# The local mask copied on another engine, and a new order for the first 400 steps

## The chip, the cores and the metric

The kernel runs on one core of one Trainium2 chip. The metric is the device time of one execution in microseconds (us), the median of several runs. The core has five engines that each work through their own queue in order: TensorE (PE, matrix products and transposes into PSUM; its weight loads are shown apart as PEld), VectorE (DVE), ScalarE (ACT), GpSimd (POOL, which reads and writes SBUF only) and SyncE (SP, which here issues nearly all DMA transfers). They wait for each other through semaphores.

## The reference

Two layers. The first is attention over 8 batches, 8 heads, 576 tokens, head size 64: heads 0 to 3 see the last 32 tokens (`mask_local`), heads 4 to 7 every 32nd token before them (`mask_strided`). The second is a mixture of four causal attention experts over the result `x` (512 wide); each token uses its best two.

```python
scores = scale * np.matmul(q, k.transpose(0, 1, 3, 2))
mask_local = (rel >= 0) & (rel < stride)
mask_strided = (rel >= 0) & (pos[None, :] % stride == pos[:, None] % stride)
attn = softmax(np.where(mask, scores, -1e9)); x = attn @ v
logits = x @ w_gate; topk = the best 2 of 4 experts; w = softmax of those two
for e in range(E):
    q, k, v = x @ wq[e], x @ wk[e], x @ wv[e]
    a = softmax(causal(scale * q @ k.T)); ye = a @ v @ wo[e]
    out += w(e) * ye
```

## The kernel before, in words

The program is a list of 2579 steps (`op(...)`, each with a kind, the engines that may do it, what it reads and writes, and a function that issues its instructions). `schedule()` issues them in the order that the list `ORDER` gives; a step that two engines can do goes to the second of them if its number is in `SECOND`. Since every engine works in order, `ORDER` sets the queue of each engine, SP's too. `FILL` gives some step numbers a count of filler matmuls (L305, 512 columns into a free PSUM bank, nobody reads them), issued on PE just ahead of that step. What stands ahead of `schedule()` (masks, zeroing, L355 to L400) is placed into the queues by the program's own scheduler, between the steps.

The first layer works on pairs of heads (`stage1(b, hp)`): pairs 0 and 1 are local, 2 and 3 strided. Batch 0 starts cold. For one local pair of batch 0 the steps are: load q and k (SP, L537, 288 KB each); transposes on PE into a bank (`tp`: four for q, four for k at L611, two for the last block of both at L624); ten copies of these banks into `qkt` (`tp_out`, L345, ACT or DVE); 72 score matmuls (`sl`, L673), which need all ten copies; then for each head mask (DVE L703, adds `m_loc`), maximum (DVE L714), subtract (POOL L716), exp (ACT L718), sum (DVE L720); reciprocal (DVE L723, L725); scale (POOL L727); a transposition on DVE (`ptl`, L743); the value products (`xal`, PE L783, needs v, loaded by L589); and a split into a rounded part and a rest (`xh` ACT L765, `xl` DVE L767). A strided pair is alike, with `tp` at L640, scores `s` at L689, `pt` on PE at L753 and value products `xa` at L802. The copies of one head and one operand write interleaved columns of `qkt`, so a later one waits for an earlier one even on another engine.

The second layer multiplies `x` with the weights: `pj` (L977 in batch 0 for the first two experts, in parts of three matmuls, each part for one pair; L966 otherwise), `vp` (L895); the weights are loaded, rounded (`hi_w`, ACT L455) and the rest taken (`lo_w`, POOL or DVE, L457).

Step numbers: 0 to 4 are GpSimd's fills (causal mask, swapped mask, last rows, two lists of zero pads). Pair 0 of batch 0: 5, 6 load q and k; 7 `tp` of q with copies 8 to 11; 12 `tp` of k with copies 13 to 16; 17 the last block with copies 18, 19; 20, 21 load v; 22 `sl`; 23, 24 mask; 25, 26 maximum; 27, 28 subtract; 29, 30 exp; 31, 32 sum; 33 reciprocal; 34, 35 scale; 36 `ptl`; 37 `xal`; 38 to 45 the split; 46, 47 small copies (`xf`). Pair 1 is the same from 48 on (48, 49 loads; 50, 55, 60 `tp`; 51 to 54, 56 to 59, 61, 62 copies; 63, 64 v; 65 `sl`; 66, 67 mask; 70, 71 subtract; 72, 73 exp; 77, 78 scale; 79 `ptl`; 80 `xal`). Pair 2 is 91 to 127 (102 `s`, 119 `xa`), pair 3 128 to 164 (134, 136, 130, 132 `tp`; 139 `s`; 153 `pt`; 156 `xa`). 165 to 203 are the weights (185 the gate's), 204 on is batch 1 (pair 0 from 204 with `tp` 206, 211, 216 and `sl` 221; pair 1 from 242 with `tp` 244, 249, 254 and `sl` 259). 1136 to 1139 and 1143 to 1146 are the eight parts of the first key projection.

The mask itself, before:

```python
for i in (0, 2, 3, 4):
    nc.vector.tensor_copy(m_loc[:, i], m_loc[:, 1])
nc.vector.memset(m_loc[0:32, 0], 0.0)
keep(m_loc[0:32, 0], [[-1, 64]], 0, 1)
```

Of the kernel before, what the change touches and what calls it, by code (L numbers as in the profile page):

```python
# [22 lines left out]
def attention_moe_kernel(  # L23
# [20 lines left out]
    nc = tc.nc  # L44
# [39 lines left out]
    class Ring:  # L84
# [36 lines left out]
    }  # L121
    ORDER = [
# [136 lines left out]
    ]  # L259
    FILL = {  # L260
        7: 1, 17: 7, 80: 4, 132: 3, 134: 3, 139: 1, 216: 2,
    }

    def op(kind, eng, key, fn, r=(), w=(), mode=None, dmas=(), after=()):
# [100 lines left out]
    m_loc = const.tile([128, 5, 64], F32, name="m_loc")  # L365
# [11 lines left out]
    for i in (0, 2, 3, 4):  # L377
        nc.vector.tensor_copy(m_loc[:, i], m_loc[:, 1])
# [916 lines left out]
```

## Time and profile before

| | |
|---|---|
| median of 3 runs | 423.1 us (422.42 to 423.28) |
| the profiled execution | 422.69 us, of which the span from first to last instruction is 421.0 us |
| mean granted TensorE clock | 0.999 |
| busy, share of the span | PE 98%, PEld 85%, DVE 81%, ACT 66%, POOL 55% |

The profiled execution's own time is 1.7 us longer than its span; that remainder lies around the program and isn't touched here. "Busy" of PE counts a matmul until its modelled end, some 0.15 us after the next may start.

### The profile page before, as it was taken

The numbers are of one execution on the slowest core, as the hardware profiler recorded it, in microseconds if no ns is written. First come the engines' busy times: TensorE is split into PE (matmuls) and PEld (weight loads), VectorE is DVE, ScalarE is ACT, GpSimd is POOL, SyncE is SP. The second block draws the span as 40 slices with busy tenths as digits, with TensorE's granted clock in tenths as the row PEclk, the third lists the DMA queues.
The fourth block names the chain that finished last, engine by engine and source line by source line (L and its number), as shares of the span: only waits on it lengthen the run. The fifth ranks groups of instructions, "written<-read, shape, count | busy, mean of one in ns | idle before, by whom it ended". The sixth has DMA issues, their size and how long they took to land.

```text
span 421.0 us, 18647 instructions
## 1 busy us (share of the span) xinstructions
PE 411.0 (98%) x7523; PEld 358.8 (85%) x7523; DVE 339.8 (81%) x1073; ACT 277.5 (66%) x877; POOL 230.3 (55%) x398
## 2 busy tenths in 40 slices
PE   8889999999999999999999999999999999999996
PEld 5668988987898879998899888998899888997775
DVE  4897898999998899978976699898988896339840
ACT  5677378668776457877767465765666469657862
POOL 5674673776536750699229630589216671185540
PEclk9999999999999999999999999999999999999999
DMA  6667637554656655464356524750443040001033
GB/s 178 194 192 181 121 91 136 100 89 96 112 102 109 146 126 87 94 129 103 72 90 133 134 46 114 129 107 11 114 102 97 20 116 22 2 26 27 27 101 100
DMA packets 156502, 41.86 MB, mean 99 GB/s; under 512 B 146080, under 2 KB 149792, under 8 KB 156416
## 3 DMA queue, kind: packets, MB, share of 16 engines
q1 hardware_dynamic: 156272, 40.54, 43.9%
q8 instruction: 59, 0.97, 1.0%
q14 instruction: 27, 0.22, 0.2%
q10 hardware_dynamic: 144, 0.13, 0.1%
HBM read 31.20 MB, written 9.44 MB: 97 GB/s over the span
## 4 chain that ended last, share of the span: by engine, by line
PE 86%; DVE 5%; ACT 3%; DMA 2%; issue 1%; POOL 1%; SPq 0%; ACTq 0%; POOLq 0%
PE bank L966 22%; PE bank L1217 12%; PE bank L1183 10%; PE bank L895 10%; PE bank L1144 6%; PE bank L1059 5%; PE bank L783 3%; PE bank L802 3%; PE bank L1047 2%; PE bank L689 2%; PE bank L673 2%; PE bank L1081 2%; PE bank L753 2%; PE bank L977 1%; DMA p<-in_q_dram 1%
## 5 line engine op out<-in xcount | busy, mean ns | idle before, releaser
L1021 ACT ACTIVATE p<-p,st 128x384 f32<-128x384 f32 (+3 forms) x128 | 71.5, 561 | 10.8 <-DVE st L1016 10.7
L1117 POOL TENSOR_SCALAR p<-p,st,wt 128x256 f32<-128x256 f32 (+2 forms) x96 | 63.9, 672 | 15.1 <-DVE st L1108 7.4
L1016 DVE CUSTOM_DVE_ANT_0 p<-bank,m_cau 128x384 f32<-128x384 f32 (+2 forms) x96 | 50.0, 548 | 1.2 <-PE bank L1059 0.6
L1183 PE MATMUL bank<-th,vs 128*64 128x192 f32 (+4 forms) x512 | 48.0, 337 | 0.0
L563 DVE STREAM_TRANSPOSE qkt<-nat 128x576 f32<-128x576 f32 x48 | 47.5, 1002 | 0.1
L1183 PEld LDWEIGHTS bank<-th,vs 128*64 128x64 f32 x512 | 33.8, 137 | 13.8 <-issue 7.1
L345 ACT COPY th<-bank 128x256 f32<-128x256 f32 (+2 forms) x108 | 40.4, 434 | 7.6 <-PE bank L1144 7.2
L765 ACT CAST xh<-bank 128x128 fp32r<-128x128 f32 (+4 forms) x112 | 29.4, 320 | 22.3 <-PE bank L783 12.8
L966 PE MATMUL bank<-xh,wh_k 128*128 128x256 f32 (+1 forms) x120 | 36.3, 303 | 0.0
L895 PE MATMUL bank<-wh_v,xh 128*128 128x260 f32 x128 | 36.2, 283 | 0.0
L895 PE MATMUL bank<-wl_v,xh 128*128 128x260 f32 x128 | 36.2, 283 | 0.0
L966 PE MATMUL bank<-xh,wh_q 128*128 128x256 f32 (+1 forms) x120 | 36.1, 301 | 0.1
L767 DVE TENSOR_TENSOR xl<-bank,xh 128x128 fp32r<-128x128 f32 (+4 forms) x112 | 31.8, 322 | 5.3 <-ACT xh L765 5.0
L895 PE MATMUL bank<-wh_v,xl 128*128 128x260 f32 x128 | 35.9, 281 | 0.0
L966 PE MATMUL bank<-xl,wh_k 128*128 128x256 f32 (+1 forms) x120 | 35.5, 296 | 0.0
L966 PE MATMUL bank<-xh,wl_k 128*128 128x256 f32 (+1 forms) x120 | 35.5, 296 | 0.0
L966 PE MATMUL bank<-xl,wh_q 128*128 128x256 f32 (+1 forms) x120 | 35.5, 296 | 0.0
L966 PE MATMUL bank<-xh,wl_q 128*128 128x256 f32 (+1 forms) x120 | 35.5, 296 | 0.0
L1144 PEld LDWEIGHTS bank<-ident,p 64*128 64x128 f32 x800 | 30.2, 139 | 5.7 <-issue 1.3
L716 POOL TENSOR_TENSOR p1l<-p1l,st 128x640 f32<-128x640 f32 (+1 forms) x18 | 20.7, 1151 | 25.7 <-DVE st L714 25.5
L1144 PE MATMUL bank<-ident,p 64*128 64x64 f32 x800 | 33.7, 226 | 0.5 <-DVE p1l L703 0.3
L727 POOL TENSOR_TENSOR p1l<-p1l,st 128x640 f32<-128x640 f32 (+1 forms) x18 | 20.5, 1141 | 18.6 <-DVE st L725 15.2
(190 smaller groups left out, 1220.1 us busy)
## 6 DMA issues: line engine op xcount, KB each, us to landing
nat<-in_q_dram SPq DMA_DIRECT2D x96, 72.0 KB
nat<-in_k_dram SPq DMA_DIRECT2D x96, 72.0 KB
out_dram<-ys SPq DMA_DIRECT2D x23, 256.0 KB
v<-in_v_dram SPq DMA_DIRECT2D x96, 40.0 KB
out_dram<-ys SPq DMA_DIRECT2D x25, 128.0 KB
v<-in_v_dram SPq DMA_DIRECT2D x48, 54.0 KB
v<-in_v_dram SPq DMA_DIRECT2D x32, 48.0 KB
v<-in_v_dram SPq DMA_DIRECT2D x32, 45.0 KB
```

Source lines behind the costliest of these rows:

```text
L345: (nc.scalar.copy if e == "ACT" else nc.vector.tensor_copy)(dst, src)
L563: op("tq", {"DVE": 0.66 if local else 1.11}, k0 - 13, lambda e, x=x: nc.vector.transpose(turned(qkt.t, x), raw(x) if local else raw(x).rea ...
L765: op("xh", {"ACT": act(n_) + 0.04 * (not local)}, key, lambda e, s_=s_, x_=x_: nc.scalar.copy(x_(xh.t), s_(xa.t)), r=[xa], w=[xh[u]])
L767: op("xl", {"DVE": dve(n_)}, key + 0.5, lambda e, s_=s_, x_=x_: nc.vector.tensor_sub(x_(xl.t), s_(xa.t), x_(f(xh.t))), r=[xa, xh[u]], w=[x ...
L895: nc.tensor.matmul(vp.t[:, :NV], xx.t[:, t0:t0 + 128], ww.t[:, kt, :], start=i == 0, stop=i == 11)
L966: nc.tensor.matmul(pj.t[:, :n_], ww.t[:, kt, ep * 128:(ep + 1) * 128], xx.t[:, c], start=i == 0, stop=i == 11)
L1016: op("max2", {"DVE": 0.08 + 0.00104 * nk}, k_ + 0.5, lambda e, a=a: nc.vector.tensor_tensor_reduce(out=p.t[:, a, :nk], in0=sp[a].t[:, so:s ...
L1021: op("exp2", {"ACT": 0.285 + 0.00084 * nk}, k_ + 1, lambda e, a=a: nc.scalar.activation(p.t[:, a, :nk], p.t[:, a, :nk], AF.Exp, bias=st.t[ ...
L1117: lambda e, p=p, a=a, ci=ci, t=t, nk=nk, s_=s_, ep=ep: nc.gpsimd.tensor_scalar(p.t[:, a, :nk], p.t[:, a, :nk], s_.t[:, 20 + ci + a:21 + ci ...
L1144: nc.tensor.transpose(tp[hf].t[:, 64 * c:64 * c + 64], src, ident[r, r])
L1183: nc.tensor.matmul(acc.t[o, c0:c0 + cn], vw, th[ep, a].t[:, s0:s0 + cn], start=j == 0, stop=j == nj - 1, skip_group_check=True)
L1217: nc.tensor.matmul(yp.t[:, :n_], xx.t[:, c0:c0 + 128], ww.t[:, ep, c], start=i == 0, stop=i == 5)
```

## The change

Three things. GpSimd, not VectorE, makes the copies of the local mask: one copy of 64 columns, one of 192 columns (three blocks at once), and the memset. The order is another one up to about position 400 of the list (after that the two lists differ only in neighbours that swap places, up to position 980), with other engines for some steps in that stretch. The 21 fillers stand ahead of other steps.

```diff
     ORDER = [
-        3, 48, 49, 50, 55, 57, 59, 60, 56, 62, 58, 52, 54, 185, 5, 7, 61, 53, 9, 51, 8, 64, 6, 17, 19, 63, 12, 13,
-        16, 0, 11, 65, 66, 68, 70, 18, 67, 15, 129, 134, 10, 14, 69, 135, 72, 22, 136, 71, 73, 137, 128, 132, 133,
-        74, 92, 91, 130, 131, 1, 139, 24, 23, 26, 28, 97, 98, 95, 99, 25, 27, 29, 75, 76, 205, 93, 211, 215, 30,
-        96, 140, 141, 143, 20, 77, 78, 79, 145, 142, 31, 144, 32, 33, 35, 34, 147, 100, 149, 146, 148, 94, 80, 87,
-        150, 151, 81, 83, 84, 82, 212, 165, 168, 213, 214, 36, 204, 216, 217, 102, 166, 104, 106, 103, 88, 152,
-        153, 167, 154, 206, 208, 155, 210, 85, 86, 105, 218, 21, 37, 42, 43, 38, 44, 243, 249, 169, 1144, 40, 41,
-        45, 108, 107, 138, 156, 242, 209, 39, 110, 112, 253, 109, 111, 161, 1136, 1137, 251, 250, 113, 157, 158,
+        3, 2, 49, 55, 58, 56, 48, 50, 53, 59, 54, 51, 60, 62, 61, 6, 12, 13, 52, 57, 65, 67, 63, 66, 68, 0, 4, 70,
+        15, 69, 5, 7, 8, 11, 9, 17, 18, 10, 19, 72, 74, 64, 16, 129, 134, 135, 92, 71, 73, 75, 76, 77, 78, 136,
+        137, 14, 22, 23, 24, 25, 27, 79, 128, 130, 131, 205, 132, 133, 139, 211, 212, 97, 26, 99, 141, 143, 28, 98,
+        145, 140, 142, 144, 1, 30, 32, 80, 87, 29, 31, 33, 146, 148, 215, 21, 91, 93, 95, 147, 149, 100, 150, 185,
+        94, 96, 213, 83, 35, 34, 36, 102, 104, 88, 84, 152, 204, 103, 105, 214, 85, 165, 168, 151, 153, 81, 82,
+        166, 167, 155, 20, 37, 106, 206, 216, 169, 40, 41, 243, 249, 38, 39, 86, 1137, 44, 42, 154, 45, 209, 107,
+        109, 138, 156, 1144, 43, 111, 1136, 1143, 108, 110, 112, 253, 113, 115, 210, 217, 250, 218, 159, 160, 208,
...
     FILL = {
-        7: 1, 17: 7, 80: 4, 132: 3, 134: 3, 139: 1, 216: 2,
+        65: 4, 93: 2, 102: 4, 130: 1, 134: 6, 139: 1, 153: 3,
     }
...
-    for i in (0, 2, 3, 4):
-        nc.vector.tensor_copy(m_loc[:, i], m_loc[:, 1])
-    nc.vector.memset(m_loc[0:32, 0], 0.0)
+    nc.gpsimd.tensor_copy(m_loc[:, 0], m_loc[:, 1])
+    nc.gpsimd.memset(m_loc[0:32, 0], 0.0)
+    nc.gpsimd.tensor_copy(m_loc[:, 2:], m_loc[:, 1:2].to_broadcast([128, 3, 64]))
     keep(m_loc[0:32, 0], [[-1, 64]], 0, 1)
```

The changes of `SECOND` give these steps another engine. Copies of transposed banks go from ACT to DVE: 10, 18, 51, 56, 58, 61, 100, 135, 137, 251, 252, 253 and four later ones; from DVE to ACT: 8, 13, 16, 53, 118, 208, 210, 245, 248 and three later ones. `lo_w` of 172, 174, 190 and 197 goes from POOL to DVE. The key's rounded copies (`k_h`) 1141, 1148, 1180 and 1184 go from ACT to POOL, `k_l` 1142 from DVE to POOL. Five small copies out of PSUM go from DVE to ACT.

## Rows read from the trace of the kernel before

**Rows 1.** Busy time per stretch: engines in order, granted clock, DMA share, GB/s.
```profile
5.00:30.00 25.00, 22.08 (x571) 15.86 (x573) 20.53 (x59) 18.78 (x54) 14.87 (x34) 1.00 0.67 188
10.00:30.00 20.00, 17.23 (x547) 12.73 (x534) 18.43 (x51) 14.89 (x45) 13.16 (x26) 1.00 0.66 188
30.00:60.00 30.00, 29.76 (x628) 27.73 (x607) 25.71 (x72) 16.74 (x50) 17.94 (x31) 1.00 0.63 142
60.00:350.00 290.00, 288.66 (x5578) 256.39 (x5565) 255.44 (x779) 195.55 (x629) 164.23 (x254) 1.00 0.49 100
```

**Rows 2.** Timeline of the first 13 us: start, length, engine, line, [idle before, releaser].
```profile
1.71 0.43 SPq L469 DMA_DIRECT2D w_gate<-in_moe_w_gate_dram  x1
...
2.18 0.51 SPq L537 DMA_DIRECT2D p<-in_q_dram  x1
2.73 1.87 SPq L589 DMA_DIRECT2D v<-in_v_dram  x4
...
3.91 1.94 PE L611 MATMUL bank<-ident,p 128*128 128x128 f32 x8
...
6.01 0.54 DVE L378 COPY m_loc<-m_loc 128x64 f32<-128x64 f32 x4 [3.24 <-POOL m_loc L362]
...
6.79 0.78 PE L611 MATMUL bank<-ident,p 128*128 128x128 f32 x4
6.92 0.23 POOL L362 TENSOR_SCALAR_AFFINE_SELECT m_loc<-m_loc 32x64 f32<-32x64 f32 x1
...
7.41 1.67 PE L305 MATMUL bank<-ident 128*128 128x512 bf16 x7
...
8.42 2.68 DVE L345 COPY qkt<-bank 64x256 f32<-64x256 f32 x6 [1.81 <-ACT qkt L345]
...
9.80 0.97 PE L673 MATMUL bank<-qkt 64*32 64x64 f32 x72
...
12.32 1.54 POOL L716 TENSOR_TENSOR p1l<-p1l,st 128x320 f32<-128x320 f32 x2 [5.18 <-DVE st L714]
```

**Rows 3.** Timeline, PE and DVE: where the later steps of the start begin.
```profile
11.96 1.39 PE L673 MATMUL bank<-qkt 64*32 64x64 f32 x72 [0.15 <-ACT qkt L345]
...
16.36 1.33 PE L640 MATMUL bank<-ident,nat 108*128 108x108 f32 x12
...
18.21 0.85 DVE L743 STREAM_TRANSPOSE pt<-p1l 128x640 f32<-128x640 f32 x1 [0.32 <-POOL p1l L727]
...
19.74 1.11 PE L783 MATMUL bank<-pt,v 32*64 32x32 f32 x84 [0.64 <-ACT qkt L345]
...
21.63 0.81 PE L689 MATMUL bank<-qkt 64*54 64x54 f32 x44
...
26.56 0.42 PE L977 MATMUL bank<-xh,wh_k 128*128 128x320 f32 x1
...
29.70 0.97 PE L673 MATMUL bank<-qkt 64*32 64x64 f32 x72 [0.46 <-ACT qkt L345]
...
34.56 0.97 PE L673 MATMUL bank<-qkt 64*32 64x64 f32 x72 [0.18 <-DVE qkt L345]
```

**Rows 4.** Groups by line and shape, DVE, ACT and POOL, 0 to 30 us.
```profile
L345 DVE COPY qkt<-bank 64x256 f32<-64x256 f32 x9 | 3.8, 426 | 2.1 <-ACT qkt L345 1.8
L703 DVE TENSOR_TENSOR p1l<-bank,m_loc 128x320 f32<-128x320 f32 x4 | 1.8, 482 | 0.0
L345 ACT COPY qkt<-bank 64x256 f32<-64x256 f32 x19 | 7.8, 417 | 5.3 <-PE bank L611 4.4 <-DVE qkt L345 0.6
L716 POOL TENSOR_TENSOR p1l<-p1l,st 128x320 f32<-128x320 f32 x4 | 2.8, 722 | 5.9 <-DVE st L714 5.8
```

**Rows 5.** Groups by line and shape, POOL, the whole span: the nearest row to the mask's copies.
```profile
L821 POOL CAST xfh<-xh 128x64 fp32r<-128x64 f32 x18 | 4.1, 235 | 10.9 <-ACT xh L765 10.9
```

**Rows 6.** Timeline around the one `lo_w` that DVE does before 60 us.
```profile
35.89 0.74 POOL L457 TENSOR_TENSOR wl_q<-th,wh_q 128x256 fp32r<-128x256 f32 x1 [3.96 <-ACT wh_q L455]
...
36.09 0.82 DVE L457 TENSOR_TENSOR wl_q<-th,wh_q 128x256 fp32r<-128x256 f32 x1
```

174 rows, old and new, of tables (ORDER, SECOND) are left out of this document.

## The prediction

> **What bounds the kernel now.** I read the busy time per stretch first [rows 1]. From 60 to 350 us PE is idle 1.34 us of 290, from 30 to 60 us 0.24 of 30: there PE sets the time, and as the change leaves its products alone, nothing can be won in that part. The cold start is different: from 5 to 30 us PE is idle 25.00 − 22.08 = 2.92 us, and in the same stretch stand the 21 fillers. So the question is only how much useful PE work each version has done when PE becomes saturated near 30 us; a lead or a lag at that point is handed down to the end. The ceiling of a gain is those 2.92 us.
>
> In the start DVE is the engine behind PE's waits: 18.43 of 20 us busy between 10 and 30 us [rows 1], the rest being hardly more than the hops between 51 groups. ACT and POOL have slack. The timeline of the first microseconds [rows 2] shows why DVE comes late: it stands for 3.24 us, until 6.01, at the mask's copies, which wait for POOL's selects, and then at its first copy out of PSUM, which waits 1.81 us for an ACT copy of the same head. The first scores run at 9.80 us, the first subtract at 12.32.
>
> **The change, part by part.** I follow the new queues step by step with these durations [rows 4]: copy 0.43 on DVE, 0.42 on ACT; mask, maximum and sum 0.48 (0.42 to the next DVE start, as they overlap), subtract and scale 0.72, a hop to another engine 0.05. A filler takes 0.215 to the next start (7 in 1.67 with the last one's tail [rows 2]), a strided `tp` 0.33 (four in 1.33 [rows 3]), a local one 0.47 when the start is over.
>
> *The mask.* VectorE loses 0.54 us of copies and a memset of 0.11 [rows 2]. In the order of before this would give nothing: DVE would only stand longer at the copy that starts at 8.42. In the new order DVE is wanted from 4.95 us, when k of pair 1 (now loaded and transposed first) is through its four transposes (half of the 1.94 us from 3.91 [rows 2]). With the mask still on DVE its copies would begin at 6.01 + 0.54 + 0.11 = 6.66, 1.7 us later; so here the edit is a condition for the new order. On POOL the copies aren't in the trace. From below: 0.235 each, the POOL row for 64 columns [rows 5]; from above the 0.72 of a two-input operation of 320 columns [rows 4]. I take 0.24 and, for three times the columns, 0.45, with 0.11 for the memset as on DVE. POOL ended the mask at 7.15 [rows 2]; the five fills of step 2, at 0.235 each 1.2 us, may now stand ahead of it, so it ends at 7.15 + 0.8 + 1.2 = 9.15, or 9.9 with the upper price for both copies. It is wanted at 9.46 (below). Value taken: nothing, being nearest to the 64-column row.
>
> *The head.* PE has both operands of pair 1 through at 5.85 [rows 2]. DVE copies 58 and 56 at 4.95 and 5.38; ACT 53 and 59 from 5.89 to 6.73; DVE 54 and 51 to 6.80; ACT 62 to 7.08; DVE 61 to 7.15. Then ACT comes to 13, which needs k of pair 0. This load is third on SP now, in the place at 1.71 of the gate's weights, 0.47 us earlier than the load at 2.18 that PE waited for until 6.79 [rows 2]; like that one it has a v load right behind it: 6.3 us. Its `tp` ends about 7.1, ACT does 13, 52, 57 until 8.39, and the scores of pair 1 start at 8.44: 1.36 us earlier than 9.80. Mask, mask, maximum on DVE from 9.46, subtract on POOL at 10.95 instead of 12.32. The head wins 1.4 us, and pair 1's chain wins more: exp at 11.7, its scale ends 15.6, the transposition on DVE starts 15.9 instead of 18.21, the value products 18.1 instead of 19.74 [rows 3].
>
> *What pays for it.* Pair 0 waits. Its q is loaded behind a v load, its `tp` runs after the first scores (9.4 to 10.05), and the last two copies stand on ACT behind pair 1's two exps: its scores start at 13.6 instead of 11.96 [rows 3], and six fillers and two `tp` cannot fill PE to there (1.1 us idle). The strided pair 3 follows at 16.15, before 15.61. Pair 2's scores need copies that stand on ACT behind pair 1's `xh` and two exps and on DVE behind sums: 22.25 instead of 21.63 [rows 3], 1.0 us idle. After that pt of pair 3 at 24.1, `xal` of pair 0 at 24.5 (0.2 earlier than before), and the first `pj` at 27.15, behind an `xl` that DVE reaches last, instead of 26.56 [rows 3].
>
> *The balance.* At the scores of batch 1's pair 0 I get 30.15 against 29.70 [rows 3], but with one `pj` part and one `tp` more done ahead of them (0.50 + 0.24 us): a lead of 0.29. At the scores of pair 1 35.45 against 34.56, with one `pj` part (0.50) more done: a lag of 0.39, since ACT does two `xh` ahead of the copy that they need. Until the last parts of the key's projection 0.12 of it comes back (a `tp` of 0.33 is done by then, where before it follows): **a lag of 0.27 us**, say 0.3. The fillers are 21 in both, so they cancel as far as PE has no other work; the loads up to there are the same number.
>
> *After 37 us.* The work on POOL's `k_h` and on ACT isn't on PE's path as long as 30 to 60 us has 4.3 us of DVE, 13.3 of ACT and 12.1 of POOL idle [rows 1]. Four more `lo_w` go to DVE. The only one that it did before took 0.82 us, beside a POOL operation that began 0.20 us earlier and ended 0.54 us after it started [rows 6]; DVE's other time for 256 columns is 0.43. So they add 1.7 to 3.3 us to DVE, and I take the cover of 4.3 us as enough: nothing. The Trainium skill, "SBUF — State Buffer", section "SBUF: two separate sides", says that VectorE and GpSimd share one pair of SBUF ports as an exclusive lock, and that a VectorE instruction with two SBUF inputs blocks while a GpSimd instruction that reads SBUF holds it. The trace agrees: 0.82 less the 0.54 leaves 0.28 of work. By that rule the four would cost DVE the upper price whenever POOL is busy; without it the lower.
>
> The sum, against the profiled execution: 422.69 + 0.3 = 423.0 us. That execution lies 0.41 below the median of 423.1, so for a median I say 423.4.
>
> **The rivals.** What a measurement of this kernel can tell from no change is about 0.2%, 0.85 us.
>
> *The head's gain lasts (faster).* If pair 0's scores and pair 2's don't leave PE empty, because their loads and copies come a little earlier than I walk them, the two idle stretches of 1.1 and 1.0 us shrink. For it: DVE starts 3.5 us earlier, and the ceiling of 2.92 us leaves room. Against: the ACT queue, where 14 stands behind both exps whatever DVE does. With 1.4 us kept less the 0.27 of the walk's end and some fillers left without a free bank: 423.1 − 1.4 = 421.7; both stretches gone, 421.3. It decides if pair 2's scores start before 21.2 us.
>
> *DVE runs out of cover (slower).* By the shared SBUF access of [rows 6] the four `lo_w` take 0.82 each, 3.3 us, in the stretch from 36 to 50 us, where the value weights must be ready before the `vp` products. DVE has 14% idle between 30 and 60 us [rows 1], 2.0 us in 14. The excess of 1.3 us and the 0.3 of the sum stand in PE's way: 423.1 + 1.6 = 424.7. It decides if PE waits over 0.5 us for `lo_w` between 36 and 50 us.
>
> *The mask comes late (slower).* If POOL takes 0.72 for each of the five fills and both copies, the mask is ready at 7.15 + 3.6 + 1.55 = 12.3 instead of 9.46, and pair 1's chain slides by 2.8 us; half of that is hidden, since pair 0's scores wait for other copies: 423.4 + 1.4 = 424.8. It decides from 10.3 us on, and is seen as DVE idle at L703 with POOL as releaser. The Trainium skill, "GPSIMD Engine Reference", section 4.1, calls GpSimd roughly line-rate on one input and about twice as slow on two. No more than that is needed to make the 0.72 too high for copies; but the row of 0.235 for 64 columns [rows 5] beside DVE's four such copies in 0.54 [rows 2] makes it 1.7 times as slow on one input too.
>
> **How the numbers follow.** The walk has some thirty hand-overs, each good to 0.1 us, and two landing times that no row gives; I put its error at 1.2 us either way, and this makes the chances. The forecast (within 0.85 us of 423.1): 0.40. The head's gain lasts: 0.32. DVE out of cover: 0.18; mask late: 0.04; and 0.06 that the walk is simply too kind to ACT's queue, with another 1 us of wait (424.4). So faster 0.32, same 0.40, slower 0.28. The range reaches from 421.3 to 425.0 and leaves 0.1 on either side. As cases of both signs hold more than half of the chance, the likeliest one's own range: 422.3 to 423.9.
>
> **What would show it.** Scores of pair 1 at 8.4 us and the first subtract at 10.95: the head is right. DVE copies from 4.95 us, no wait for m_loc on DVE. Pair 0's scores at 13.6 behind ACT copies; pair 2's at 22.25; first `pj` at 27.15. PE idle in 5 to 30 us of 3 to 4 us, a little more than 2.92, and from 30 to 60 us under 1 us. Wrong would make me: a granted clock below 1.00 after the longer PE gaps, a DMA that lands late (k of pair 0 after 7 us), POOL's fills between the first subtracts, or PE idle of more than 1 us past 36 us.

## Result and the profile after

The changed kernel takes 427.81 us (median of six executions, 424.24 to 428.87) against 422.76 for the kernel before, timed beside it: a ratio of 1.0107 (95% interval 1.0083 to 1.0131). The forecast was 423.4 with a range to 425.0; the change made the kernel 5 us slower. (One of the six executions took 424.24, with a mean granted clock of 1.000 where the other five have 0.990 to 0.996: it had neither of the two falls of the clock described below. It has no trace, so whether it also escaped the long wait of VectorE is open.) The profiled execution took 428.07 us, with a span of 426.4 and a mean granted clock of 0.991 (before 421.0 and 0.999).

To see where the time went I take two products of the second half whose instructions are the same in both kernels and read their starts in the PE timeline. Before:

```profile
243.88 0.50 PE L783 MATMUL bank<-pt,v 32*64 32x32 f32 x33
...
300.56 0.45 PE L783 MATMUL bank<-pt,v 32*64 32x32 f32 x26
```

And after:

```profile
245.40 0.43 PE L783 MATMUL bank<-pt,v 32*64 32x32 f32 x24
...
305.99 0.43 PE L783 MATMUL bank<-pt,v 32*64 32x32 f32 x24
```

The changed kernel is 1.52 us late at the first and 5.43 at the second. So there are two losses: **1.5 us at the start, and 3.9 more between 244 and 306 us**, in a part that the change hardly touches. The busy time per stretch finds both (columns as in [rows 1]):

```profile
5.00:30.00 25.00, 21.17 (x536) 15.11 (x536) 19.95 (x53) 15.12 (x42) 15.68 (x41) 0.93 0.65 177
...
20.00:25.00 5.00, 3.27 (x50) 1.77 (x50) 3.17 (x11) 3.69 (x11) 4.15 (x8) 0.73 0.61 156
25.00:30.00 5.00, 5.00 (x157) 3.95 (x156) 4.51 (x15) 2.66 (x9) 1.77 (x3) 0.93 0.50 156
30.00:60.00 30.00, 29.02 (x564) 26.84 (x564) 24.96 (x67) 19.00 (x59) 16.13 (x18) 1.00 0.66 144
60.00:280.00 220.00, 218.23 (x4356) 195.07 (x4356) 195.82 (x600) 152.34 (x493) 125.00 (x202) 1.00 0.54 106
...
290.00:300.00 10.00, 7.55 (x148) 6.14 (x145) 8.49 (x18) 4.45 (x15) 5.79 (x10) 0.83 0.09 20
300.00:350.00 50.00, 49.97 (x947) 43.82 (x945) 43.48 (x138) 29.83 (x96) 22.78 (x33) 1.00 0.32 81
```

PE is idle 3.83 us from 5 to 30 us (2.92 before) and 2.45 us from 290 to 300. At both places the granted clock falls, each time behind a wait of PE of 2 us or more. In 20 to 30 us the two means make 5 x 0.27 + 5 x 0.07 = 1.7 us lost, that is 3.4 us at the lower level of 1.2 GHz; in 290 to 300 again 10 x 0.17 = 1.7.

**The first loss** in the timeline of PE, with the VectorE copy that ends the wait:

```profile
8.01 0.95 PE L673 MATMUL bank<-qkt 64*32 64x64 f32 x70 [0.27 <-ACT qkt L345]
...
13.26 0.95 PE L673 MATMUL bank<-qkt 64*32 64x64 f32 x70 [1.36 <-ACT qkt L345]
...
17.52 1.11 PE L783 MATMUL bank<-pt,v 32*64 32x32 f32 x84
18.56 0.60 PE L305 MATMUL bank<-ident 128*128 128x512 bf16 x2
19.00 0.72 PE L640 MATMUL bank<-ident,nat 108*128 108x108 f32 x6
21.73 1.33 PE L305 MATMUL bank<-ident 128*128 128x512 bf16 x4 [2.02 <-DVE qkt L345]
22.99 1.37 PE L689 MATMUL bank<-qkt 64*54 64x54 f32 x44
...
21.20 0.48 DVE L345 COPY qkt<-bank 128x324 f32<-128x324 f32 x1
```

Up to 19 us the prediction's walk holds. Then four fillers ahead of pair 2's scores find no free bank until VectorE's copy 100 has ended; PE stands for 2.02 us, four fillers and the scores run behind it at the lower clock (the 44 score matmuls take 1.37 instead of 0.81 in [rows 3]), and pair 2's scores come at 22.99.

**The second loss** begins on VectorE at 287.31 us, at the first comparison of the gate of batch 5 (L920, both operands in SBUF, 64 columns; eight such per execution, median 0.22 us). VectorE and GpSimd, after:

```profile
287.31 5.39 DVE L920 TENSOR_TENSOR gt<-vs 128x64 f32<-128x64 f32 x1
292.63 0.39 DVE L921 TENSOR_TENSOR eq<-vs 128x64 f32<-128x64 f32 x1
...
293.42 0.48 DVE L989 TENSOR_TENSOR qkr<-bank,qkr 128x320 fp32r<-128x320 f32 x1
...
287.25 0.77 POOL L1117 TENSOR_SCALAR p<-p,st,wt 128x512 f32<-128x512 f32 x1
287.97 0.39 POOL L997 CAST qkr<-qk 128x256 fp32r<-128x256 f32 x1
288.34 0.81 POOL L1123 TENSOR_SCALAR p<-p,st,wtl 128x576 f32<-128x576 f32 x1
289.13 1.26 POOL L727 TENSOR_TENSOR p1s<-p1s,st 128x648 f32<-128x648 f32 x1
290.36 0.72 POOL L1001 TENSOR_TENSOR qkr<-qk,qkr 128x256 fp32r<-128x256 f32 x1
291.07 1.40 POOL L1117 TENSOR_SCALAR p<-p,st,wt 128x384 f32<-128x384 f32 x2
292.46 0.48 POOL L1117 TENSOR_SCALAR p<-p,st,wts 128x128 f32<-128x128 f32 x1
...
293.95 0.86 PE L1144 MATMUL bank<-ident,p 64*128 64x64 f32 x19 [2.45 <-DVE qkr L989]
```

The comparison lasts 5.39 us, across seven GpSimd operations that follow each other without a gap. Everything behind it on VectorE waits, so also the subtraction of L989, which PE waits for; PE stands for 2.45 us, and then the clock falls: 2.45 + 1.7 = 4.15, of which 3.9 are left. The same comparison before:

```profile
286.03 0.60 DVE L920 TENSOR_TENSOR gt<-vs 128x64 f32<-128x64 f32 x1
```

### The profile page after: what moved, and what is told of

Same layout as the page of the kernel before. It is cut to its first block, busy times and chain, and to the rows that moved or that the text cites. A ratio compares the mean times of both kernels' runs of the same rounds, so it can differ in the third digit from the quotient of the medians.

```text
span 426.4 us, 18632 instructions
## 1 busy us (share of the span) xinstructions
PE 411.8 (97%) x7523; PEld 359.9 (84%) x7523; DVE 344.6 (81%) x1071; ACT 275.8 (65%) x873; POOL 230.8 (54%) x402
## 4 chain that ended last, share of the span: by engine, by line
PE 60%; DVE 5%; SPq 1%; issue 1%; DMA 1%; ACT 1%; DVEq 0%; ACTq 0%
PE bank L966 15%; PE bank L1217 10%; PE bank L1183 8%; PE bank L895 6%; PE bank L1144 5%; PE bank L1059 4%; PE bank L783 2%; PE bank L802 2%; PE bank L1047 2%; PE bank L1081 2%; PE bank L673 1%; PE bank L689 1%; PE bank L865 1%; DVE gt L920 1%; PE bank L753 1%
## 5 line engine op out<-in xcount | busy, mean ns | idle before, releaser
L1117 POOL TENSOR_SCALAR p<-p,st,wt 128x512 f32<-128x512 f32 (+2 forms) x96 | 63.7, 670 | 16.2 <-DVE st L1108 7.6
L1183 PE MATMUL bank<-th,vs 128*64 128x192 f32 (+4 forms) x512 | 49.5, 344 | 0.0
L765 ACT CAST xh<-bank 128x160 fp32r<-128x160 f32 (+4 forms) x112 | 29.4, 320 | 27.2 <-PE bank L783 16.0
L1183 PEld LDWEIGHTS bank<-th,vs 128*64 128x64 f32 x512 | 34.7, 140 | 14.4 <-issue 6.8
L966 PE MATMUL bank<-xh,wh_q 128*128 128x320 f32 (+1 forms) x120 | 36.2, 302 | 0.1
L966 PE MATMUL bank<-xh,wl_q 128*128 128x320 f32 (+1 forms) x120 | 35.5, 296 | 0.0
L966 PE MATMUL bank<-xl,wh_q 128*128 128x320 f32 (+1 forms) x120 | 35.5, 296 | 0.0
```

Of the source, the lines that this page charges most:

```text
L765: op("xh", {"ACT": act(n_) + 0.04 * (not local)}, key, lambda e, s_=s_, x_=x_: nc.scalar.copy(x_(xh.t), s_(xa.t)), r=[xa], w=[xh[u]])
L966: nc.tensor.matmul(pj.t[:, :n_], ww.t[:, kt, ep * 128:(ep + 1) * 128], xx.t[:, c], start=i == 0, stop=i == 11)
L1117: lambda e, p=p, a=a, ci=ci, t=t, nk=nk, s_=s_, ep=ep: nc.gpsimd.tensor_scalar(p.t[:, a, :nk], p.t[:, a, :nk], s_.t[:, 20 + ci + a:21 + ci ...
L1183: nc.tensor.matmul(acc.t[o, c0:c0 + cn], vw, th[ep, a].t[:, s0:s0 + cn], start=j == 0, stop=j == nj - 1, skip_group_check=True)
```

## Experiments

Times are medians beside the kernel before on the same chip (422.4 to 422.7). The lag of a run below is the start of the product of 243.88 and of 300.56 us, less these, each in the one profiled execution of the run.

**Does the comparison cost the time, and which operation is shut out?** `gate_move` puts step 2002 (the comparison and its two followers) 31 steps later; `mask_dve` gives VectorE its mask copies back and leaves all else as in the changed kernel.

```diff
 gate_move, ORDER of after
-  2111, 1929, 1928, 2002, 1954, ... 2122, 2123, 923, 2125,
+  2111, 1929, 1928, 1954, ... 2122, 2123, 923, 2002, 2125,
 mask_dve
-    nc.gpsimd.tensor_copy(m_loc[:, 0], m_loc[:, 1])
-    nc.gpsimd.memset(m_loc[0:32, 0], 0.0)
-    nc.gpsimd.tensor_copy(m_loc[:, 2:], m_loc[:, 1:2].to_broadcast([128, 3, 64]))
+    for i in (0, 2, 3, 4):
+        nc.vector.tensor_copy(m_loc[:, i], m_loc[:, 1])
+    nc.vector.memset(m_loc[0:32, 0], 0.0)
```

> The changed kernel with one step elsewhere in the order: the gate's comparisons of batch 5 (the VectorE step whose first comparison took 5.39 us beside a run of GpSimd instructions) are issued 31 places later, behind a sum of batch 6. Theory 1 (VectorE's comparison, which reads two SBUF operands, is shut out by GpSimd's unbroken run, and PE and the rest wait for it): the 4.1 us of lag that arise between 287 and 296 us go, and the time falls from 427.8 to about 423.7; the lag of 1.3 to 1.5 us from the start stays. Theory 2 (those 4 us come from something that the start left late, a load or a bank, and the comparison only waited with it): the time stays at 427 to 428. Theory 3: the next VectorE instruction with two SBUF operands (the rest of the key) is shut out in its place, 425 to 428 with a long instruction at that line.

> The changed kernel with the copies of the local mask back on VectorE (order, engines and fillers as changed). By the prediction's step VectorE's first copy out of PSUM starts at about 6.7 instead of 5.02, pair 1's scores 0.3 to 0.8 later than 8.0, its chain as much later. Rival: VectorE has slack before 9 us (it waited 1.68 us for the mask on GpSimd), so the scores come 0.5 later but the mask no later than now, and the lag at 60 us is the same within 0.3.

`gate_move`: 427.26 us, ratio 1.0107 (1.0093 to 1.0121). The victim changes: the next VectorE operation with two SBUF operands, the rest of a key (L1001; five lines later in this kernel), is shut out in its place, as theory 3 had it.

```profile
287.65 5.72 DVE L1006 TENSOR_TENSOR qkr<-qk,qkr 128x320 fp32r<-128x320 f32 x1
```

The profiled execution also shows what the wait costs without a fall of the clock. PE stands for 1.98 us, the clock stays at 1.00 behind it, and the lag grows by 2.24 us (1.71 to 3.95) instead of 3.9:

```profile
290.00:300.00 10.00, 8.02 (x170) 6.81 (x168) 10.00 (x22) 5.43 (x18) 6.31 (x10) 1.00 0.14 30
```

So of the 3.9 us some 2.2 are the wait and some 1.7 the clock, which is what the means of 290 to 300 us gave.

`mask_dve`: 423.91 us, ratio 1.0040 (1.0026 to 1.0054). In its profiled execution (425.05 us) the start is worse (lag 2.11 at the first product), yet the median is 3.9 us below that of the changed kernel, as no operation is shut out (lag 1.98 at the second product):

```profile
288.01 0.61 DVE L920 TENSOR_TENSOR gt<-vs 128x64 f32<-128x64 f32 x1
```

So the second loss is a meeting of VectorE and GpSimd at 287 us, and the place of the mask's copies, 280 us earlier, is enough to take it away. At the start itself that place is worth half a microsecond: VectorE's first two copies out of PSUM go ahead of the mask's copies (5.02 us in both), and pair 1's first mask runs at 9.53 instead of 9.06.

**Can it be avoided?** `gate_kl` is `gate_move` with that rest of the key on GpSimd too (step 1973 put into `SECOND`), so that no such operation is left there.

> The changed kernel with the gate's comparisons of batch 5 issued 31 places later, as in gate_move, and with the next VectorE instruction that reads two SBUF operands there (the rest of batch 5's key, which took 5.72 us in gate_move) given to GpSimd, so that VectorE has no such instruction beside GpSimd's run near 288 us. Theory (VectorE is shut out by the run): no VectorE instruction above 1.5 us there, the lag of 4.1 us goes, 423.5 to 424.5. Rival (the lag at 287 us comes from what the start left late): 427 to 428 as before, with another wait in that place.

425.09 us, ratio 1.0052 (1.0038 to 1.0066); no VectorE operation is long, and the lag is 1.79 at the first product and 2.26 at the second. The 3.9 us have become 0.5. That shows the price of the second loss a second time. The time is 0.6 us above the theory's range, with a start that lags by 1.79.

**What does the start cost, and why?** `nofill102` drops the four fillers; `copy100` puts VectorE's copy 100 earlier, behind 99; `early14` is `gate_kl` without the fillers and with ACT's copies 14 and 16 right behind 15; `before_mask_pool` is the kernel before with the changed kernel's three GpSimd lines.

```diff
 nofill102, early14
-        65: 4, 93: 2, 102: 4, 130: 1, 134: 6, 139: 1, 153: 3,
+        65: 4, 93: 2, 130: 1, 134: 6, 139: 1, 153: 3,
 copy100, ORDER of after
-  97, 26, 99, 141, ... 147, 149, 100, 150,
+  97, 26, 99, 100, 141, ... 147, 149, 150,
 early14, ORDER of after
-  70, 15, 69, ... 64, 16, 129, ... 137, 14, 22,
+  70, 15, 14, 16, 69, ... 64, 129, ... 137, 22,
```

> The changed kernel without the four fillers ahead of pair 2's scores (17 fillers in all). Theory A1 (what costs is that the fillers wait for a bank and then run at a falling clock ahead of the scores): scores start at 22.0 instead of 22.99, lag at 60 us about 1 us less, though PE's gap grows to 2.3 us and the half clock stays. Theory A2 (the clock is what costs, and fillers at whatever place shorten it): the half clock comes as early or earlier, lag unchanged or up to 0.5 larger.

> The changed kernel with one copy of a transposed bank of pair 2 (VectorE) issued right behind its transposes, 26 places earlier, so that the bank comes free for the fillers ahead of pair 2's scores. Theory A (PE's gap of 2.02 us at 19.7 us is a wait for that bank, and it brings 3.4 us at half clock): gap and half clock go, pair 2's scores start near 22.0 instead of 22.99 and run 0.8 instead of 1.37 us, the lag at 60 us falls from 2.0 to about 0.5; time 1.5 less. Theory B (PE would wait anyway, for the copies on ACT and VectorE): scores at 22.5 to 23, lag unchanged within 0.4. The 4 us at 287 us may come or not; the lag at 60 us is what tells.

> gate_kl, and two edits of the start: no fillers ahead of pair 2's scores, and the two last copies of pair 0's key bank (ACT) issued right behind the first, ahead of pair 1's exps. Theory (pair 0's scores wait 1.36 us for these copies, pair 2's scores 1 us for the fillers, and both go to the end): pair 0's scores start near 12.0 instead of 13.26 us, the lag at 60 us falls from 2.0 to between -0.3 and 0.3, time 422.0 to 423.0. Rival (VectorE's queue holds the start up, the copies are not the last to arrive): pair 0's scores earlier, but the lag at 60 us still about 1.0 as without the fillers alone, 423.3 to 424.

> The kernel before with the copies of the local mask on GpSimd, nothing else changed. The prediction's step: worth nothing in that order, because VectorE's first copy out of PSUM waits for an ACT copy until 8.42 us: 422.2 to 423.2, the first scores at 9.8. Rival: the copies on GpSimd delay its other fills and the mask, and the lag at 60 us is 0.3 to 1.0.

| | us | ratio (95%) | lag at 243.88 | at 300.56 |
|---|---|---|---|---|
| `nofill102` | 427.68 | 1.0127 (1.0106 to 1.0147) | 0.56 | 4.49 |
| `copy100` | 428.46 | 1.0129 (1.0095 to 1.0163) | 2.09 | 7.15 |
| `early14` | 424.47 | 1.0039 (1.0025 to 1.0053) | 1.12 | 1.33 |
| `before_mask_pool` | 423.17 | 1.0012 (1.0002 to 1.0023) | 0.68 | 0.61 |

A lag from one execution is good to some 0.7 us only: `late_256_256` below, the kernel before up to 286 us, reaches the first product at 243.17, 0.71 ahead of the kernel before, and it was already 0.74 ahead at pair 0's scores (11.22 for 11.96). The five profiled executions with the changed start and all its fillers lag by 0.58 to 2.47.

Without the fillers the profiled start is 1.0 us better, but the median is that of the changed kernel: PE's wait only passes to the scores themselves.

```profile
21.77 1.55 PE L689 MATMUL bank<-qkt 64*54 64x54 f32 x44 [2.12 <-DVE st L723]
```

`copy100` lets the four fillers run early and leaves 1.59 us of idle time, but the scores start no sooner (23.28, behind an ACT copy). `early14` removes pair 0's wait of 1.36 us, and pair 2's scores still come at 22.24 with 2.46 us idle; with its lag of 1.12 it comes near the rival (about 1.0), not the theory. None of the three edits brings these scores much ahead of 22 us. So it isn't one filler or one copy that holds the start; that it is the queues of ACT and VectorE as a whole, where the copies for pair 2 stand behind exps and sums, is likely but not shown. The mask's copies on GpSimd alone lose about half a microsecond in the old order (0.1 to 1.0 by the interval), where the prediction had nothing.

What the fall of the clock costs at the start is seen in one more pair. The kernel `after_late_64` (below) is the changed one up to 287 us. In its profiled execution PE waits the same 2.02 us, but the clock stays at 1.00 (first the busy time per stretch, then PE's timeline):

```profile
20.00:25.00 5.00, 2.98 (x64) 1.63 (x62) 3.90 (x13) 4.02 (x12) 4.09 (x9) 1.00 0.64 200
```

```profile
22.07 1.02 PE L305 MATMUL bank<-ident 128*128 128x512 bf16 x4 [2.02 <-DVE qkt L345]
23.03 0.81 PE L689 MATMUL bank<-qkt 64*54 64x54 f32 x44
...
244.46 0.38 PE L783 MATMUL bank<-pt,v 32*64 32x32 f32 x17
```

Its lag at the first product is 244.46 - 243.88 = 0.58 us, against 1.52, although its start as a whole is 0.34 us later (the fillers at 22.07 instead of 21.73, pair 0's scores at 13.60 instead of 13.26). From these fillers to the product it takes 222.39 us, the changed kernel with its fall of the clock 223.67; `gate_move`, `gate_kl` and `after_late_256_256`, which all have the fall, take 223.65 to 224.05. So the fall costs 1.3 us here, up to 1.7 in one of the others, and of the start's 1.52 us only 0.2 are left as lost work. The means above gave 1.7; but PE is idle 1.73 us from 20 to 30 us with the fall and 2.14 without it, and the difference of 0.4 explains the rest. The times of `mask_dve` agree: its four executions with a mean granted clock of 0.998 or 0.999 take 423.73 to 423.91 us, its three with 0.994 or 0.995 take 425.05 to 425.19, 1.1 to 1.5 more.

**Both repairs together.** `kl_nofill` is `gate_kl` without the four fillers, `mask_dve_nofill` is `mask_dve` without them.

> The changed kernel with both repairs: without the four fillers ahead of step 102 (worth 1.0 us at 60 us when taken out alone), and with the comparison 2002 moved and 1973 on GpSimd (worth 2.2 to 2.8 us alone). Theory: two causes in different places, so the gains add: 427.3 less 1.0 less 2.2 to 2.8, 423.5 to 424.1 us, 0.8 to 1.4 above the kernel before; no VectorE operation of two SBUF operands over 1.5 us. Rival: the second loss depends on where the stages meet, so an earlier start shifts another such operation into GpSimd's run, and 426 to 427.5 remain.

> The changed kernel with the mask's copies back on VectorE and without the four fillers ahead of step 102. With the fillers and the mask on VectorE it was 423.91. Theory: the fillers cost 1.0 us at the start here too and VectorE meets GpSimd's run near 287 us at another moment than in the changed kernel, so no operation is shut out: 422.6 to 423.3, no better than the kernel before. Rival: the 1 us by which the stages then come earlier brings the comparison back into the run, as in the changed kernel whose start lies 0.5 us earlier: 426 to 427.5, with a VectorE operation of over 5 us near 287.

`kl_nofill` 424.73 us (1.0042, 1.0029 to 1.0055), `mask_dve_nofill` 424.59 (1.0051, 1.0034 to 1.0068). Neither has a long VectorE operation, as the theories said, but the microsecond of the fillers didn't come, and both times miss their ranges: the first product comes 0.52 us earlier than in `gate_kl` and no earlier than in `mask_dve`, so the gain of 1.0 in `nofill102` is not a price of the fillers. Both wait 2.0 to 2.1 us at pair 2's scores and have the fall of the clock behind it (lags of 1.27 and 2.12 at the first product). No version beat the kernel before.

**Why does it last so long?** First a small program: runs of 2 to 16 GpSimd operations on one tile, and a VectorE comparison (64 columns) that meets them after 64 to 448 columns of copies.

> Not the kernel: a small program that writes zeros to the output, and on the side runs trials. In each, GpSimd does a run of n instructions on SBUF, and VectorE, after a copy out of PSUM of 64 to 448 columns, one instruction: a comparison of two SBUF tensors of 64 columns (0.2 us alone), or an instruction that reads PSUM and one SBUF tensor, or one SBUF tensor alone. Theory (exclusive use of what the two engines share, and GpSimd's next instruction takes it again without a gap): the comparison beside a run lasts until the run's end, about (n - 1) x 0.8 us, in some or all delays, and grows with n; the one with PSUM and the reduction of one tensor stay at 0.2. Rival 1 (it waits for one instruction at most): 0.2 to 1.0 us whatever n. Rival 2 (no sharing): 0.2 us always.

The comparison takes 0.21 us alone and 0.28 to 0.61 beside the run, whatever its length (0.51 with 2, 4 and 16 operations), and up to 1.23 beside operations of 1.6 us: one operation at most. Beside the same run an operation on PSUM and one SBUF tensor takes 0.21 us and a reduction of one tensor 0.21, and the comparison beside memsets 0.21; but a copy from SBUF to SBUF takes 0.48, so VectorE operations with two SBUF operands are not the only ones that wait. The same with operations on different tiles, in the kernel's mix (`probe2`), and met in steps of 8 ns (`probe3`, `probe4`, the latter with ScalarE copies and a transfer beside it):

> A small program that leaves the whole computation out: GpSimd runs of ten or eight operations, now on different tiles, with VectorE's gate comparison (128x64 with broadcast operands in SBUF) started after 64 to 2176 columns of PSUM copies. Theory: GpSimd operations that do not depend on one another hand the SBUF on without a gap, so at some delays the comparison lasts several of them, 1.5 to 5 us, and it ends where the run ends. Rival: one GpSimd operation at most holds it here too (at most 1.4 us for the longest, 768 columns, some 0.6 for the 512-column ones), so that what shuts it out for 5.4 us in the kernel is something that this program lacks.

> A small program that leaves the whole computation out: GpSimd's eleven operations as they stand around 287 us of the changed kernel (256, 256, rest 256, 512, cast 256, 576, 648, rest 256, 384, 512, 128 columns, on different tiles), and VectorE's gate comparison started in steps of about 8 ns around the beginning of the 512-column operation that follows the rest, then of the cast, and around the second operation of a run of eight 512-column ones. In the four kernels where an operation was shut out it began 0.02 to 0.06 us after that 512-column operation; in those where it was not, it began 0.2 us into the rest or met no run. Theory: what shuts it out is this meeting within some 0.06 us of a beginning; then some of these starts last 3 to 5.5 us. Rival: also here one operation at most, up to 0.95 us beside 512 columns, so the meeting alone does not do it and what the kernel adds (waits between the engines, transfers, the other engines' accesses) stays open.

> A small program that leaves the whole computation out: the same eleven GpSimd operations and the gate's comparison as in the last one, whose steps met the 512-column operation only 0.3 us after its beginning. Now 25 starts in steps of 8 ns run from the end of the rest over the beginning of the 512-column operation, and the same 25 once more with ScalarE copying from SBUF and a transfer reading it meanwhile. Theory: the comparison that begins 0.02 to 0.06 us after that operation is shut out for several operations, 3 to 5.5 us, in one of the two series. Rival: one operation at most in both, so the moment of meeting is not enough by itself in a program this small, and what else the kernel adds stays open.

One operation at most again, in all 124 comparisons; the longest is 1.50 us, beside one of 1.47:

```profile
99.36 1.47 POOL L46 TENSOR_TENSOR big<-big,st 128x768 f32<-128x768 f32 x1
99.41 1.50 DVE L71 TENSOR_TENSOR res<-vs 128x64 f32<-128x64 f32 x1
```

In the kernel, four shut-out operations had begun 0.02 to 0.06 us after the same GpSimd operation, so I moved the comparison by fills of an unused tile: in the kernel before (`late_256_256`, `late_256_256_64`) and in the changed one (`after_late_64`, `after_late_256_256`).

```diff
+            for n in (64,) if b == 5 else ():
+                nc.vector.memset(spare[:, :n], 0.0)
             nc.vector.tensor_tensor(gt.t[:, :nt], l_f, l_e, ALU.is_gt)
```

> The kernel before, with two fills of 256 columns of an unused tile ahead of the gate's comparison of batch 5, so that VectorE comes to it some 0.4 to 0.55 us later than in the kernel before (there it began 0.24 us into GpSimd's rest, 0.48 us ahead of the 512-column operation). Theory: the moment of meeting alone decides; if the comparison then begins 0.02 to 0.07 us after that operation, it lasts over 5 us and the time is 426 to 427 without any change of the start. At another moment (before it, or more than 0.1 us after it) 0.2 to 0.9 us and 422.6 to 423.2. Rival: the changed start is needed for it (another state of buffers or transfers), and the kernel before never shows it: at most 0.9 us wherever it begins.

> The same with a third fill of 64 columns, some 0.1 us later still. Theory: over 5 us and 426 to 427 only if the comparison begins 0.02 to 0.07 us after the 512-column operation, which one of these two should come near; otherwise 0.2 to 0.9 us. Rival: at most 0.9 us in any case.

> The changed kernel with one thing more: a fill of 64 columns of an unused tile on VectorE ahead of the gate's comparison of batch 5, so that it begins some 0.1 to 0.2 us later, 0.15 to 0.3 us into GpSimd's 512-column operation instead of 0.06. Everything up to 287 us stays as it is, the start with its lag of 1.5 too. Theory: it is the moment of meeting to a tenth of a microsecond; the comparison then waits for one operation at most (0.2 to 0.8 us), the 4.1 us are gone and the time is 423.3 to 424.0. Rival: GpSimd's unbroken run as such shuts out what comes into it; the comparison still lasts about 5 us and 427 to 428 remain.

> The same with two fills of 256 columns, some 0.55 us later, near the end of the 512-column operation or in the cast behind it. Theory: as above, 423.5 to 424.3, unless it comes within 0.1 us of a beginning again. Rival: still over 4 us, and 427 to 428.

Before: 422.51 and 422.50 us (0.9997 and 1.0002), the comparison 0.16 and 0.83 us long; it began 0.17 and 0.37 us into the operation, so these two did not hit the moment. Changed: 428.58 and 427.81 us (1.0158 and 1.0141). The first only moved it to 0.14 us into the operation, the second to the end of it, 0.03 us after the cast behind it began:

```profile
286.59 5.31 DVE L922 TENSOR_TENSOR gt<-vs 128x64 f32<-128x64 f32 x1
```

```profile
288.95 4.72 DVE L922 TENSOR_TENSOR gt<-vs 128x64 f32<-128x64 f32 x1
```

The first refutes my theory of the moment. The second proves less, as it met a beginning again, the case that its expectation excepted. Both are shut out until the same GpSimd operation of 128 columns begins: this speaks for GpSimd's run. What tells the two kernels apart is seen ten microseconds ahead, at another VectorE operation with two SBUF operands, one of four columns (L930; the line number shifts in some variants). Before, it begins 0.08 us after a GpSimd operation and lasts 1.21 us beside it; so its result comes late, and GpSimd waits for VectorE twice a few microseconds later:

```profile
277.25 1.21 DVE L930 SCALAR_TENSOR_TENSOR wt<-sel,wt 128x4 f32<-128x4 f32 x1
...
277.17 1.26 POOL L716 TENSOR_TENSOR p1l<-p1l,st 128x640 f32<-128x640 f32 x1
278.92 0.20 POOL L940 TENSOR_TENSOR wt<-wt,mx 128x4 f32<-128x4 f32 x1 [0.49 <-DVE mx L932]
...
281.08 0.82 POOL L1123 TENSOR_SCALAR p<-p,st,wtl 128x576 f32<-128x576 f32 x1 [0.33 <-DVE wtl L345]
```

After, it begins 0.15 us ahead of that GpSimd operation and lasts 0.20 us. GpSimd's two come without a wait, and the run goes on from 275.99 to 292.94 us with no pause in which GpSimd waits for another engine:

```profile
278.61 0.20 DVE L930 SCALAR_TENSOR_TENSOR wt<-sel,wt 128x4 f32<-128x4 f32 x1
...
278.76 1.26 POOL L716 TENSOR_TENSOR p1l<-p1l,st 128x640 f32<-128x640 f32 x1
279.98 0.20 POOL L940 TENSOR_TENSOR wt<-wt,mx 128x4 f32<-128x4 f32 x1
...
281.81 0.81 POOL L1123 TENSOR_SCALAR p<-p,st,wtl 128x576 f32<-128x576 f32 x1
```

The other traces agree. Twelve of the kernel's traces have a VectorE operation with two SBUF operands near 287 us. In six (the kernel before, `before_mask_pool`, `mask_dve`, `mask_dve_nofill` and the two `late` runs) the operation of L930 lasts 1.20 to 1.23 us, GpSimd has the two waits, and nothing is shut out. In the six others (the changed kernel, `gate_move`, `nofill102`, `copy100` and the two `after_late` runs) it lasts 0.20 to 0.21, GpSimd has no wait, and one operation is shut out for 4.72 to 5.72 us. The lag doesn't tell them apart: -0.71 to 2.12 at the first product in the former, 0.56 to 2.47 in the latter. Nor does the place in the GpSimd operation: begun 0.17 us into it the comparison takes 0.16 us (`late_256_256`), begun 0.14 us into it 5.31 (`after_late_64`). That GpSimd's pause is what lets VectorE in is argued from this, as no run changes the pause alone, and what puts the operation of L930 ahead of GpSimd's or behind it was not followed back to the start.

So the last small program (`probe5`) meets long runs late.

> A small program that leaves the whole computation out. In the kernels with the long comparison GpSimd has worked without a wait for about 10 us when the comparison comes (in the changed kernel from 277.4 on); in the kernel before and with the mask on VectorE it waited 0.33 us for VectorE 5 us ahead of it, and in the small programs so far the comparison came in the first 2.5 us of a run. So here the runs are 20 to 24 us long without a wait, and one comparison comes 2.5 to 18 us after the beginning. Theory: a run that has gone on for 5 us or more lets no VectorE operation of two SBUF operands in; the late starts last 2 us and more. Rival: one GpSimd operation at most (0.2 to 1.3 us), however long the run has gone on, so that the length of the run isn't it either, and the mechanism stays open.

Of its 28 comparisons 25 waited for one operation at most, 17 of them in the kernel's mix up to 22 us into the run. But three of the eight in runs of thirty 512-column operations on nine tiles, begun 9.9 and some 15 us after the run's start, were shut out for several:

```profile
473.76 22.62 POOL L44 TENSOR_SCALAR big<-big,one 128x512 f32<-128x512 f32 x30 [0.33 <-ACT ps L67]
483.65 7.74 DVE L76 TENSOR_TENSOR res<-vs 128x64 f32<-128x64 f32 x1
...
511.54 2.97 DVE L76 TENSOR_TENSOR res<-vs 128x64 f32<-128x64 f32 x1
...
534.95 2.67 DVE L76 TENSOR_TENSOR res<-vs 128x64 f32<-128x64 f32 x1
```

Each passed as the 24th operation began: with one operation each 22.62 / 30 = 0.754 us, 23 of them end 17.3 us after the run's start at 473.76, at 491.1, and the comparison ends at 491.39. So a run of GpSimd operations can shut VectorE out for ten of them, outside this kernel too. A long run is not enough for it (25 of 28), and what opens the gap at one operation and not at the ten before it is still open.

## Why the prediction was wrong, step by step

- **The mask: right, but not a condition.** GpSimd's copies took 0.24 and 0.35 us (estimated 0.24 and 0.45) and VectorE's first mask ran at 9.06. With the copies on VectorE it ran at 9.53: half a microsecond, not the 1.7 us by which VectorE's start was to slide.
- **The head: right.** Scores of pair 1 at 8.01 (8.44), the first subtract at 10.62 (10.95), the value products at 17.52 (18.1).
- **What pays for it: right in place, short in size.** Pair 0's scores wait 1.36 us (1.1) and begin at 13.26 apart from two early ones (13.6); PE's idle time from 5 to 30 us is 3.83 ("3 to 4"). But pair 2's scores wait 2.0 us where the walk had 1.0.
- **The balance: the first step that failed, by a term that it lacked.** The fall of the granted clock behind PE's wait, named as something that would make the forecast wrong, was given no price; it cost 1.3 us. Measured 1.52 against 0.27. What is left without the fall, 0.2 (0.6 in the profile without it), agrees with the 0.27, but in part by luck: the value products came 0.6 us earlier than in the walk and pair 2's scores 0.7 later (22.99 for 22.25). That the fillers cancel "as far as PE has no other work" did not hold for the four ahead of step 102: they had no bank until 21.68 and stood in the scores' way.
- **"A lead or a lag at that point is handed down to the end": the step that cost most, with "After 37 us ... nothing".** The lag was not handed down; it grew from 1.5 to 5.4 us near 290 us. The shared access of VectorE and GpSimd was priced for the four `lo_w` alone, and these were indeed harmless: from 30 to 60 us PE is idle 0.98 us in all, in no wait of over 0.5. But every VectorE operation with two SBUF operands may meet a GpSimd run, and a change of the start can turn such a meeting round. One went from 0.60 to 5.39 us, and it made 3.9 of the 5.4 us: 2.2 by PE's wait and 1.7 by a second fall of the clock. The two falls together are 3.0 of the 5.4 us. The Trainium skill, "SBUF — State Buffer", section "SBUF: two separate sides", says that the one of the two that starts first keeps the pair for the whole instruction. The trace agrees that the comparison stands behind GpSimd, but not that one instruction is the measure: here it was seven in a row, in the small program ten.
- **The rivals.** The head's gain did not last; the mask was not late; VectorE's cover did not run out where that rival put it.

That VectorE is shut out, that this costs 2.2 us and with the fall of the clock about 4, and that the mask's place is enough to decide whether it happens, are shown by `gate_move`, `gate_kl` and `mask_dve`. Why GpSimd keeps the access over several operations here and lets VectorE in at each boundary elsewhere is not settled.

## What to carry to other kernels

A change of the start can turn round every later meeting of two engines that share a resource, whatever the size of the lag; in the profile before, look for operations whose longest instance is a multiple of their median (here VectorE's with two SBUF operands, beside unbroken GpSimd runs), as each is a price that may be drawn again. Taking such operations off VectorE there removed the loss (`gate_kl`); a pause in the GpSimd run may do it too, but no run tried that. A wait of 2 us on PE can cost more than its length, since the clock may fall behind it (1.3 and 1.7 us here): give it that price with a chance, and give no fillers to a place where they must wait for a bank that the next product needs.

## What was unexpected

- VectorE's comparison of 64 columns, 0.21 us alone, lasted 5.39 us over seven GpSimd operations in the kernel and 7.74 us over ten in a small program; met in steps of 8 ns elsewhere it never waited for more than one.
- A VectorE operation of four columns that waits 1 us for GpSimd at 277 us goes together with a gain: in the six traces where it waits, GpSimd pauses and nothing is shut out ten microseconds later.
- The fall of the granted clock is not bound to the wait alone: after the same wait of 2.02 us on PE it fell to the lower level for 3.4 us in one execution and stayed at 1.00 in another, which makes 1.3 us at the first product.
